# Softmax sums inverted on VectorE in the last blocks of a fused attention and feed-forward kernel, with the order of the last five blocks written anew

## The chip, the cores and the metric

The kernel runs on one core of a Trainium2 chip. The metric is device time in microseconds of one execution; of several runs the median is taken. Each core has TensorE (PE, matrix products into PSUM), ScalarE (ACT, functions such as the exponential), VectorE (DVE), GpSimd (POOL) and SyncE (SP, which here issues most DMAs). Each engine works through its own instructions strictly in the order in which the program lists them; semaphores make one wait for another.

## The reference

```python
x = A_x                                   # 1 x 2048 x 448, bf16
xn = _layernorm(x)                        # no scale, no shift
qkv = xn @ A_wqkv                         # 16 heads of 28
p = softmax(q @ k.T * 28 ** -0.5)         # per head, 2048 x 2048
s = (p @ v) @ A_wo
h = gelu(xn @ B_w1 + B_b1)                # 1792 wide
g = silu(h @ B_w2 + B_b2)
return x + s * g
```

There are 16 x 2048 x 2048 exponentials, and they are the bulk of the work.

## The kernel before

The sixteen heads form four groups `g` of four, and the 2048 queries four chunks `c` of 512. A pair (g, c) is a *block*; `ORD` lists the sixteen blocks in the order in which they run, numbered 0 to 15. A block has 64 *pieces*, one for each head of the group and each of the 16 key tiles of 128 keys: a score matmul (`t_score`, line 1430) makes a 128x512 piece in one PSUM bank, and ScalarE takes the exponential of two or three pieces in neighbouring banks at once (`p_exps`, line 1486). A second matmul (line 1866, from `t_pv`) multiplies each exponentiated piece by the values `vaug`, which carry an extra column that yields the softmax sums, and adds it up in the one PSUM bank `acc` that a block has. Block 15 is handled in three parts of 256, 128 and 128 queries by functions of its own (`p_epi4`, `p_norm4`, `p_last`).

ScalarE does not make all exponentials. Some key tiles of a block (only those listed in `VT`, eight at most for each block) are taken as *late quads*, four pieces at a time: VectorE makes an approximate exponential by integer arithmetic on the bits (`p_apass`, line 1715), then two shifted copies of the four pieces (`p_expq`, line 1774), and the three are weighted with `vaug` and with scaled values `vs` in the second matmul. If a setting allows it, GpSimd first adds the two shifted copies (line 1787, four additions); the quad is then *merged*, and needs fewer matmuls. `NQ` gives for each block how many tries are made to take a late quad; a try comes to nothing when the piece is already too near.

When a block is finished, `p_epi` copies `acc` to SBUF in `E_sb` (line 1929, VectorE). The 4x512 sums then travel through DRAM so that they lie as 128x16 in `rs` (lines 1941 and 1943; for block 14 four direct DMAs, line 1938). GpSimd inverts them into `rc` with the power -1 (line 1945). `rc` goes back through DRAM (line 1947) and is spread over the partitions by four DMAs (line 1950) into `rb`, and GpSimd multiplies `E_sb` by it (line 1954), giving the normalized block in `qT`. All those DMAs are issued by SP. The output projection of a chunk (line 1964) needs all four groups of it; its results are multiplied by the gate on VectorE (line 1981), and leave with an accumulating DMA from GpSimd (line 1990) or, for the last chunks, after an addition of x on VectorE (line 1985) by SP (line 1987). The feed-forward part runs between the blocks: first layer (line 1278), GELU in one stretch (line 1326), second layer (line 1347) with its bias added at line 1353, and SiLU as a tanh on ScalarE (line 1363) with products on GpSimd (lines 1368 and 1370) or VectorE (line 1374).

The order of all this is made by a planner in the file itself, while the program is being built. Each step is a `_Task` with an engine, a reckoned duration and latency, and a priority; `run` always takes the step that can begin first by this reckoning, with priorities among those that begin at nearly the same time. A DMA is reckoned to land a `lag` after its issue: 4.0 us each for the steps of an epilogue, and `LAG` for blocks 12 and later. Nothing of the reckoned times is in the program, only the order on each engine and the waits. `BP` holds seventeen rows of twenty settings, named in `BPN`; `tune` loads a row when the first scores of a block are listed. Among them are `MG` (1: late quads may be merged on GpSimd), `PV0` and `PVC` (how far the second matmul may fall behind), `ND4` and `LQ` (how many quads may be under way), `JMAX` (how many late pieces may join a score group), `QLEAD` and `QDIST` (how long before its use a quad may or must be taken), `UR` and `SLACK` (urgency on TensorE) and `R3` (whether groups of three scores are made; at 4 the banks 2 and 3 of the ring are kept for them).

Of the kernel before, what the change touches and what calls it, by code (L numbers as in the profile page):

```python
# [8 lines left out]
ALU = mybir.AluOpType  # L9
ET = mybir.EngineType  # L10

PE, ACT, DVE, POOL, SP = ET.PE, ET.Activation, ET.DVE, ET.Pool, ET.SP
# [38 lines left out]
)  # L51
NQ = (5, 11, 13, 13, 12, 7, 11, 10, 16, 3, 16, 15, 12, 13, 12, 14)
QLEAD, QDIST = 0, 12
JMAX, DQ, LQ, ND4, LU = 2, 3, 2, 3, 3
PV0, PVC, MP = 12, 4, 0.3
# [35 lines left out]
PVN = 2  # L91
OWN2 = 0
EA = 0
LAG, ONS = 3.0, 1.0
LNR = 1
G3P = 0
PATH = {(1, 2): 'D', (1, 3): 'D', (2, 0): 'D', (2, 1): 'D', (2, 2): 'D', (2, 3): 'D'}
# [30 lines left out]
class _Kernel:  # L128
# [1457 lines left out]
    def p_late(self):  # L1586
# [4 lines left out]
        for b in range(NBLK):  # L1591
            i = 0
            while True:
                if i:
                    K.nq_read = b
                at = 64 * b - QLEAD + (i * (64 - QDIST) // NQ[b] if i else 0)
                yield ("until", lambda: K.next_m >= at)
                K.nq_read = b
                if i >= NQ[b]:
                    break  # L1600
# [323 lines left out]
    def p_epi(self, b):  # L1924
        K = self
        g, c = ORD[b]
        E = K.E_sb[:, b % 2, :]
        tE = K.b_E[b % 2]
        yield _Task(DVE, lambda eng: eng.tensor_copy(E, K.acc[:, :]), [K.b_acc], [tE], 0.7, 0.0, 0)
        K.E_done = b  # L1930
        K.copying = False
        yield ("until", lambda: K.late_on)
        lag = LAG if b >= NBLK - 4 else 4.0
        src = bass.AP(tensor=K.E_sb, offset=DH * 1024 + 512 * (b % 2), ap=[[32 * 1024, 4], [1, 512]])
        if b == NBLK - 2:
            for j in range(4):
                one = bass.AP(tensor=K.E_sb, offset=(32 * j + DH) * 1024 + 512 * (b % 2), ap=[[1024, 1], [16, 32], [1, 16]])
                K.dma(SP, lambda eng, j=j, one=one: eng.dma_start(K.rs[32 * j:32 * j + 32, :], one), K.s_r[1],
                      reads=[tE], writes=[K.b_srs] if j == 3 else [], land=max(K.now, tE.tw) + lag)
        else:  # L1940
            K.dma(SP, lambda eng: eng.dma_start(K.sums.ap(), src), K.s_r[0], reads=[tE], writes=[K.b_sums],
                  land=max(K.now, tE.tw) + lag)
            K.dma(SP, lambda eng: eng.dma_start(K.rs[:, :], K.sums.ap().rearrange("j (i k) -> (j i) k", k=16)), K.s_r[1],
                  reads=[K.b_sums], writes=[K.b_srs], land=K.b_sums.tw + lag)
        yield _Task(POOL, lambda eng: eng.tensor_tensor(K.rc[:, :], K.rs[:, :], K.mone[:, 0:1].to_broadcast([128, 16]), ALU.pow),  # L1945
                    [K.b_srs, K.b_pads], [K.b_rc], 3.0, 0.05, 1)
        K.dma(SP, lambda eng: eng.dma_start(K.recs.ap().rearrange("j (i k) -> (j i) k", k=16), K.rc[:, :]), K.s_r[2],
              reads=[K.b_rc], writes=[K.b_recs], land=max(K.now, K.b_rc.tw) + lag)
        for j in range(4):
            h = K.dma(SP, lambda eng, j=j: eng.dma_start(K.rb[32 * j:32 * j + 32, :], K.recs.ap()[j].partition_broadcast(32)),  # L1950
                      K.s_r[3], reads=[] if j else [K.b_recs], writes=[] if j else [K.b_rb], land=0.0)
        K.mark(h, [K.b_recs], [K.b_rb], K.b_recs.tw + lag + 0.6)
        dst = K.qT[:, g, c * 512:(c + 1) * 512]
        yield _Task(POOL, lambda eng: eng.tensor_tensor(dst, K.rb, E, ALU.mult), [K.b_rb, tE], [K.b_onT[g][c]], 1.15, 0.05, 1,  # L1954
                    port=True)
        K.on_done[b] = True
# [111 lines left out]
```

## Time and profile before

| | |
|---|---|
| time, median of 3 runs | 420.60 us (420.59 to 420.64) |
| the profiled execution | 420.68 us |
| its span | 418.88 us |
| busy: PE, ACT, DVE, POOL | 396.6, 404.8, 345.0, 188.2 us |
| the power on GpSimd, line 1945 | 15 of 2.997 us in the mean, 45.0 us |
| merging additions on GpSimd, line 1787, in the last 165 us | 20, most of 1.15 us |
| copies of `acc`, line 1929, blocks 10 to 14 | end at 302.5, 322.5, 343.3, 370.1, 390.7 us |
| last exponential | ends at 411.5 us |

The span runs from the first to the last instruction of one profiled execution; its time includes what lies around the span. Lines such as `L1945 POOL TENSOR_TENSOR rc<-rs,mone 128x16` name the source line, the engine, the operation, what is written from what, and the tile. "Idle before" is time for which the engine stood still just before an instruction, with the instruction or DMA that released it. Consecutive instructions of one engine overlap in the records, so their pace is read from start to start. The busy time of a TensorE instruction is modelled.

### The profile page before, as it was taken

Reading aid. Unit: us, or ns where it says so; the run is one execution under the profiler, and the core shown is the slowest. Engines: PE = TensorE matmul, PEld = TensorE weight load, DVE = VectorE, ACT = ScalarE, POOL = GpSimd, SP = SyncE. Lnnn points to the kernel's source line nnn. Section 1 sums busy time; section 2 is a strip of 40 time slices with the busy share of each in tenths; the row PEclk is TensorE's granted clock in tenths of the full one; section 3 lists DMA queues with packets and bytes.
Section 4 is the critical chain, followed back from the end, with each engine's and each line's share of the span. In section 5 each row is a group of like instructions: output and inputs, shape, how many; then the busy total and the mean of one; then the engine's idle time right before and its main releaser. Section 6 shows DMA issues by size and latency. Waiting matters only on the chain.

```text
span 418.9 us, 9607 instructions
## 1 busy us (share of the span) xinstructions
PE 396.6 (95%) x3640; PEld 133.8 (32%) x3666; DVE 345.0 (82%) x594; ACT 404.8 (97%) x412; POOL 188.2 (45%) x193
## 2 busy tenths in 40 slices
PE   6899999999999999999999999999999999999996
PEld 4543223332222222222223443232222322323443
DVE  8968899997786899999894126799998899899387
ACT  5999999999999999999999999999999999999994
POOL 6571333237769271203331424408325618880660
PEclk9999999999999999999999999999999999999999
DMA  8701000000001000000230000000010001211052
GB/s 270 264 2 40 3 3 27 12 19 15 26 2 27 0 2 30 2 27 15 60 112 26 27 1 2 2 2 14 15 27 3 9 22 23 49 46 28 2 126 80
DMA packets 15952, 15.29 MB, mean 36 GB/s; under 512 B 7129, under 2 KB 12993, under 8 KB 15874
## 3 DMA queue, kind: packets, MB, share of 16 engines
q1 hardware_dynamic: 15042, 13.07, 10.8%
q0 software_dynamic: 576, 0.92, 1.5%
q8 instruction: 29, 0.48, 0.5%
q10 hardware_dynamic: 288, 0.69, 0.4%
q14 instruction: 17, 0.14, 0.1%
HBM read 12.59 MB, written 2.93 MB: 37 GB/s over the span
## 4 chain that ended last, share of the span: by engine, by line
PE 60%; ACT 23%; issue 8%; DVE 6%; POOL 2%; ACTq 0%; POOLq 0%; DVEq 0%
PE ring L1430 18%; PE acc L1866 13%; ACT P L1486 13%; PE ring L1278 8%; ACT h L1486 7%; PE ring L1347 7%; PE ring L923 2%; PE misc L923 2%; PE misc L1347 2%; ACT xnT L1486 2%; PE misc L1278 1%; PE ring L1217 1%; PE acc L1064 1%; PE misc L1217 1%; PE ring L1964 1%
## 5 line engine op out<-in xcount | busy, mean ns | idle before, releaser
L1486 ACT ACTIVATE P<-ring 128x1024 bf16<-128x1024 f32 (+1 forms) x238 | 252.1, 1161 | 1.8 <-PE ring L1430 0.7
L1430 PE MATMUL ring<-qT,kT 32*128 32x512 bf16 (+2 forms) x1045 | 140.9, 357 | 9.7 <-ACT P L1486 2.0
L1486 ACT ACTIVATE h<-ring 128x1024 bf16<-128x1024 f32 (+1 forms) x80 | 87.2, 1191 | 0.1
L1430 PEld LDWEIGHTS ring<-qT,kT 32*128 32x128 bf16 x1045 | 38.0, 91 | 144.0 <-ACT P L1486 81.0
L1945 POOL TENSOR_TENSOR rc<-rs,mone 128x16 f32<-128x16 bf16 x15 | 45.0, 2997 | 32.7 <-DMA rs<-sums 24.5
L1866 PE MATMUL acc<-P,vaug 128*32 128x512 bf16 (+2 forms) x618 | 54.3, 351 | 0.0
L1278 PE MATMUL ring<-xnT,w 128*128 128x512 bf16 x169 | 46.0, 381 | 1.4 <-issue 0.8
L1486 ACT ACTIVATE xnT<-ring 128x1024 bf16<-128x1024 f32 (+2 forms) x38 | 43.0, 1172 | 2.0 <-PE ring L1430 1.4
L1954 POOL TENSOR_TENSOR qT<-x_sb,E_sb 128x512 bf16<-128x512 f32 x15 | 19.6, 1304 | 51.9 <-PE acc L1866 21.2
L1347 PE MATMUL ring<-w,h 128*128 128x448 bf16 x168 | 40.5, 355 | 0.3 <-DVE vaug L1715 0.3
L1430 PE MATMUL misc<-qT,kT 32*128 32x512 bf16 (+1 forms) x107 | 40.7, 382 | 0.0
L1866 PE MATMUL acc<-h,vaug 128*32 128x512 bf16 x230 | 27.9, 384 | 0.0
L1172 POOL TENSOR_TENSOR qsq<-qT 128x512 bf16<-128x512 bf16 x12 | 12.5, 1040 | 33.2 <-DVE qT L1166 30.6
L1715 DVE TENSOR_SCALAR x_sb<-ring 128x512 uint16<-128x512 f32 x38 | 25.7, 685 | 1.7 <-PE ring L1430 1.3
L1715 DVE TENSOR_SCALAR x_sb<-misc 128x512 uint16<-128x512 f32 x30 | 20.6, 686 | 4.7 <-PE misc L1430 4.0
L1368 POOL TENSOR_TENSOR h<-w 128x448 bf16<-128x448 bf16 x12 | 12.7, 1058 | 23.8 <-DVE h L1774 14.5
L1715 DVE TENSOR_SCALAR h<-ring 128x512 uint16<-128x512 f32 x33 | 22.3, 685 | 0.0
L1278 PEld LDWEIGHTS ring<-xnT,w 128*128 128x128 bf16 x180 | 14.7, 97 | 23.8 <-issue 8.3
L1799 POOL TENSOR_SCALAR vs<-vaug 128x128 bf16<-128x128 bf16 x32 | 9.5, 297 | 21.2 <-DVE w L1774 18.6
L1866 PEld LDWEIGHTS acc<-P,vaug 128*32 128x32 bf16 x618 | 13.3, 95 | 15.1 <-issue 12.6
L1347 PEld LDWEIGHTS ring<-w,h 128*128 128x128 bf16 x168 | 12.3, 97 | 17.9 <-issue 10.6
L1262 DVE CAST h<-ring 128x512 bf16<-128x512 f32 x21 | 14.4, 685 | 4.4 <-PE ring L1278 4.3
(265 smaller groups left out, 700.4 us busy)
## 6 DMA issues: line engine op xcount, KB each, us to landing
x_sb<-recs SPq DMA_DIRECT2D x60, 64.0 KB, 2.0
w<-in_B_w_dram SPq DMA_DIRECT2D x1, 1568.0 KB, 7.2
w<-in_B_w_dram SPq DMA_DIRECT2D x1, 1344.0 KB, 8.4
x_sb<-in_A_x_dram SPq DMA_DIRECT2D x2, 448.0 KB, 4.6
out_dram<-in_A_x_dram SPq DMA_DIRECT2D x2, 448.0 KB, 9.8
out_dram<-h POOLq DMA_DIRECT2D x4, 224.0 KB, 4.4
out_dram<-h SPq DMA_DIRECT2D x8, 112.0 KB, 1.7
h<-in_A_wqkv_dram SPq DMA_DIRECT2D x3, 168.0 KB, 4.9
```

The source lines that it names most:

```text
L923: return eng.matmul(bank, w[:, k, g * 128:(g + 1) * 128], K.xnT[:, k, c * 512:(c + 1) * 512], start=(k == 0), stop=(k == KT - 1))
L1172: yield _Task(POOL, lambda eng: eng.tensor_tensor(qs, qb, qb, ALU.mult), [qr], [tq], 1.1, 0.05, 2, port=True)
L1262: yield _Task(DVE, lambda eng: eng.tensor_copy(dst, bank), [tok], wr, 0.69, 0.0, 2)
L1278: return eng.matmul(bank, K.w1[:, k, ft * 128:(ft + 1) * 128], K.xnT[:, k, c * 512:(c + 1) * 512], start=(k == 0), stop=(k == KT - 1))
L1347: ins = eng.matmul(ps, hv[:, ft, t * 128:(t + 1) * 128], K.w2[:, ft, :], start=(ft == 0), stop=(ft == FT - 1))
L1368: yield _Task(POOL, lambda eng, o=o, t=t: eng.tensor_tensor(o, sg[:, t, :], fb[:, t, :], ALU.mult), [K.b_sig[c % 2], K.b_fsb[c % 2]], [K.b ...
L1430: return eng.matmul(dst, K.kT[32 * j:32 * j + 32, g, t * 128:(t + 1) * 128], K.qT[32 * j:32 * j + 32, g, c * 512 + q0:c * 512 + q0 + nq], ...
L1486: return eng.activation(reg[:, i0:i0 + n, :], K.ring[:, b0:b0 + n, :], ACTF.Exp, scale=SM_SCALE)
L1715: yield _Task(DVE, lambda eng: eng.tensor_scalar(K.part(u, k).bitcast(dt.uint16), K.like(u, bank), SM_SCALE * LOG2E * 128.0, (127.0 - EXP_ ...
L1866: return eng.matmul(K.acc[32 * j:32 * j + 32, q0:q0 + nq], w, ap[:, col:col + nq] if len(ap.shape) == 2 else ap[:, col // 128:(col + nq) / ...
L1945: yield _Task(POOL, lambda eng: eng.tensor_tensor(K.rc[:, :], K.rs[:, :], K.mone[:, 0:1].to_broadcast([128, 16]), ALU.pow), [K.b_srs, K.b_ ...
L1954: yield _Task(POOL, lambda eng: eng.tensor_tensor(dst, K.rb, E, ALU.mult), [K.b_rb, tE], [K.b_onT[g][c]], 1.15, 0.05, 1, port=True)
```

## The change

From block 11 on (`RCB = 11`), the sums of a block are inverted by `reciprocal` on VectorE and not by the power on GpSimd; the planner reckons 0.25 us for it, with priority 2, where the power had 3.0 us and priority 1. Block 15 has an epilogue of its own and is not concerned, so four inversions move, those of blocks 11 to 14. `LAG` goes from 3.0 to 3.5, so that the planner reckons longer DMAs in the epilogues of blocks 12 to 14. The rows 11 to 15 of `BP` get other settings, and `NQ` for blocks 13 and 14 becomes 15 and 9. Since the planner's order follows from all these, the order on every engine can differ from the place on where row 11 is loaded. The computation is the same.

```diff
-    (0, 0.227, 10, 0.102, 12, 6, 0.124, 9, 17, 0.113, 1, 6, 4, 8, 1.0, 1.3, 75, 28, 0, 3.77),
-    (0, 5.612, 12, 0.137, 9, 10, 0.124, 4, 18, 0.4, 1, 4, 8, 2, 0.413, 1.275, 90, 16, 4, 5.0),
-    (1, 6.265, 18, 0.121, 15, 2, 3.663, 5, 6, 0.064, 1, 3, 8, 3, 0.519, 2.119, 60, 38, 0, 3.491),
-    (0, 2.077, 13, 0.119, 14, 3, 0.232, 9, 16, 0.334, 1, 1, 9, 12, 0.378, 1.28, 88, 16, 0, 6.0),
-    (1, 4.0, 5, 0.1, 6, 6, 0.298, 3, 18, 0.206, 1, 3, 8, 21, 0.202, 0.491, 48, 20, 2, 1.109),
+    (0, 0.186, 10, 0.156, 21, 9, 0.124, 9, 17, 0.251, 5, 6, 3, 8, 1.0, 4.428, 75, 28, 0, 3.77),
+    (1, 5.612, 31, 0.218, 9, 8, 0.059, 6, 18, 0.316, 1, 3, 8, 4, 0.682, 1.275, 98, 12, 1, 5.0),
+    (1, 6.265, 5, 0.121, 25, 10, 3.663, 5, 6, 0.064, 1, 1, 10, 3, 0.13, 2.119, 60, 38, 1, 3.491),
+    (0, 1.756, 13, 0.029, 14, 7, 0.232, 9, 16, 0.03, 1, 7, 9, 12, 0.211, 4.579, 52, 24, 0, 6.0),
+    (1, 4.0, 5, 0.1, 6, 7, 0.298, 3, 18, 0.206, 1, 3, 8, 21, 0.202, 0.491, 18, 20, 2, 1.109),
...
-NQ = (5, 11, 13, 13, 12, 7, 11, 10, 16, 3, 16, 15, 12, 13, 12, 14)
+NQ = (5, 11, 13, 13, 12, 7, 11, 10, 16, 3, 16, 15, 12, 15, 9, 14)
...
-LAG, ONS = 3.0, 1.0
+LAG, ONS = 3.5, 1.0
+RCB = 11
...
-        yield _Task(POOL, lambda eng: eng.tensor_tensor(K.rc[:, :], K.rs[:, :], K.mone[:, 0:1].to_broadcast([128, 16]), ALU.pow),
-                    [K.b_srs, K.b_pads], [K.b_rc], 3.0, 0.05, 1)
+        if b >= RCB:
+            yield _Task(DVE, lambda eng: eng.reciprocal(K.rc[:, :], K.rs[:, :]), [K.b_srs], [K.b_rc], 0.25, 0.0, 2)
+        else:
+            yield _Task(POOL, lambda eng: eng.tensor_tensor(K.rc[:, :], K.rs[:, :], K.mone[:, 0:1].to_broadcast([128, 16]), ALU.pow),
+                        [K.b_srs, K.b_pads], [K.b_rc], 3.0, 0.05, 1)
```

## The prediction

> **What bounds the kernel now.** I read the page's busy times first, then busy time by stretch, with the stretches cut where VectorE copies a finished block's sums out of PSUM (`E_sb<-acc`, line 1929).
>
> ```profile
> span 418.9 us, 9607 instructions
> PE 396.6 (95%) x3640; PEld 133.8 (32%) x3666; DVE 345.0 (82%) x594; ACT 404.8 (97%) x412; POOL 188.2 (45%) x193
> ```
> ```profile
> core 0: us, PE busy (x) PEld busy (x) DVE busy (x) ACT busy (x) POOL busy (x), PEclk, DMA share, GB/s
> 302.40:322.40 20.00, 19.98 (x181) 5.79 (x179) 19.82 (x32) 20.00 (x21) 6.96 (x5) 1.00 0.06 16
> 322.40:343.20 20.80, 19.82 (x203) 6.26 (x201) 17.54 (x27) 20.80 (x20) 10.03 (x8) 1.00 0.05 15
> 343.20:370.00 26.80, 25.89 (x207) 7.84 (x207) 24.49 (x40) 25.83 (x28) 21.13 (x18) 1.00 0.18 28
> 370.00:390.70 20.70, 20.42 (x239) 6.23 (x237) 19.20 (x33) 20.59 (x21) 8.75 (x5) 1.00 0.15 38
> 390.70:411.50 20.80, 19.70 (x347) 9.65 (x350) 12.92 (x23) 19.34 (x19) 11.16 (x8) 1.00 0.32 76
> ```
>
> ScalarE bounds it, TensorE close behind. From the place where the change begins to act (block 11, scored from about 300 us), ScalarE is idle 0.97 + 0.11 + 1.46 = 2.54 us. That is all that better ordering can win; more comes only if VectorE takes exponentials over. VectorE is idle 0.18 + 3.26 + 2.31 + 1.50 = 7.25 us in the first four stretches. POOL has room except in the third, and the granted clock is 1.00 throughout.
>
> Next the chain that ended last, at the end of block 14, and the waits in that place:
>
> ```profile
> 389.99 0.69 DVE E_sb L1929
> 390.68 0.61 DVE xnT L1774
> ...
> 392.54 1.15 POOL wk L1787
> 393.69 1.81 issue
> 395.53 2.91 POOL rc L1945
> 398.44 3.09 POOL wk L1787 x2
> 401.66 0.40 PE acc L1866 x8
> ```
> ```profile
> PE acc L1866 <- POOL wk L1787: 0.9, 1, 0.9
> ```
> ```profile
> 402.93 1.45 ACT L1486 ACTIVATE xnT<-ring 128x1536 bf16<-128x1536 f32 x1 [0.92 <-PE ring L1430]
> 409.99 1.02 ACT L1486 ACTIVATE P<-ring 128x1024 bf16<-128x1024 f32 x1 [0.38 <-PE ring L1430]
> ```
>
> The power (`rc`) stands in POOL's queue between the second and third of the four adds that merge block 15's late quad. POOL waits there 1.81 us for the DMA of the sums, works 2.91 us, then makes the other two adds. TensorE stands 0.91 us for them with the next scores queued behind, and ScalarE then idles 0.92 us. This is the one place where the power lies on the path. After 309, 329, 351 and 373 us the chain does not pass through it.
>
> How much VectorE already takes over comes from the matmuls that read the scaled values `vs`, which only late quads use: 8 for a plain quad, 4 for a merged one (columns: the stretch, busy PE with its count, weight loads, POOL).
>
> ```profile
> 302.40:321.70 19.30, 2.01 (x24) 0.54 (x24) 0.00 (x0) 1.00 0.06 17
> 322.40:342.60 20.20, 4.56 (x48) 1.16 (x48) 0.00 (x0) 1.00 0.05 16
> 343.20:369.40 26.20, 0.78 (x8) 0.21 (x8) 0.00 (x0) 1.00 0.19 29
> 370.00:390.70 20.70, 5.02 (x64) 1.70 (x64) 0.00 (x0) 1.00 0.15 38
> 390.70:411.50 20.80, 0.40 (x8) 0.15 (x8) 0.00 (x0) 1.00 0.32 76
> ```
>
> So 3, 6, 2 (merged), 8 and 1 (merged, half-width matmuls) quads in blocks 11 to 15: 20.
>
> **The change part by part.** Sums go against the profiled execution: span 418.88, time 420.68, so 1.80 around the span; that is 0.08 above the median, 420.60.
>
> *Power out of POOL.* Four of the fifteen powers go (blocks 11 to 14; block 15 has none): 4 x 3.0 = 12 us of POOL, of which 0.92 of ScalarE's idle time is on the path. Without it the four adds run from 391.43 to about 396.1 in place of 401.5, 4 us before TensorE reaches them; late next are ScalarE and TensorE themselves. **-0.92.** Between nothing and -0.92.
>
> *Earlier normalized block 14.* Its sums land at 395.5 either way. Then 0.26 in place of 2.91, the store (398.47 to 399.91 now), four broadcast loads from SP (1.71 plus some 2), and POOL's multiply, which now runs at 405.12 behind the adds and two output transfers of its queue. It can be done by about 402.5, not 406.4. The output matmuls (line 1964) that need it crowd 405.9 to 409.3, just ahead of the 0.38 idle at 409.99; spread out they let that go. **-0.38**, between -0.38 and 0.
>
> *Reciprocal on VectorE.* No 128x16 reciprocal is in the trace; 128x128 takes 948 ns, and the smallest operation near it, the 128x2 aggregate, 161. In proportion: 161 + 787 x 16/128 = 0.26 each, 1.05 for four, from 0.64 to 3.8 at the two rows. It waits in order for a DMA. For blocks 11 to 13 the sums are there 3.5 us after the copy (302.5 to 306.0 in block 10, where POOL waited only for them), and the order reckons 7 or 8, so nothing queued behind it waits. For block 14 it reckons 3.5 and the trace says 4.85, so up to 1.35 us in order. VectorE idles there 5.31 us before the line-1353 addition at 396.59. **0**; if the 7.25 us of cover are used up, +1.05.
>
> [...]
>
> *Longer reckoned transfers* (3.0 to 3.5) issue nothing new; they place the consumers later in the queues. SP's own order stays sums, reciprocals, broadcasts. **0**, by the slack above; bounds -0.4 to +0.4, the smaller of the two stalls.
>
> *Five rows anew.* Three things in them have a price. (a) Block 12 no longer keeps two banks for groups of three scores (R3 4 to 1). In 321.31 to 343.83 there are ten triples at 1.33 and ten pairs at (22.52 - 13.3)/10 = 0.92; ten triples as fifteen pairs cost +0.47, while block 13 (R3 0 to 1) may win that back. I take **+0.2**, bounds -0.47 and +0.47. The freed banks also let late scores come faster: from 330.8 to 336.0 they used one bank, 1.29 apart. (b) Block 12's quads may be merged on POOL (MG 0 to 1). A merge saves TensorE 4 matmuls, 0.22 us by the chain's step from 8 to 12 (0.55 to 0.76). For two quads -0.4 on TensorE, not on ScalarE: **0**. (c) Tries for late quads: block 13 gets 15 for 13, block 14 gets 9 for 12. One quad is 4 x 0.455 = 1.82 us of ScalarE and 6 x 0.6 = 3.6 of VectorE. The number follows from rules that the trace cannot replay: **0**, bounds -1.8 (one more fits the 7.25 idle) and +3.6 (two fewer).
>
> Sum: -0.92 - 0.38 + 0.2 = -1.10: 419.58 against the profiled time, **419.5** against the median.
>
> **The rivals.** *One quad more.* For it: VectorE's idle time, block 12's banks, and block 13 with 2 quads where blocks 12 and 14 have 6 and 8. Against: VectorE is 92 to 99% busy in the other stretches. 419.5 - 1.8 = **417.7**.
>
> *No gain.* New POOL merges in block 12 meet VectorE's shift passes (line 1774). The trace shows such meetings: 1.81 us beside an add at 354.15 where 0.68 is usual, and POOL's multiply taking 3.26 in place of 1.15 beside the shift passes that run to 388.9. Three shift passes lengthened by 1.1 eat 3.3 of the 3.26 idle in block 12's stretch, late scores come later and ScalarE loses the 1.1 again: **420.6**. [...]
>
> *Slower: quads go back to ScalarE.* Block 14 has 8 quads from 12 tries; at that rate 9 tries give 6, and block 13's 15 tries at 2 in 13 give none in return. One quad fewer is 421.3, two 423.1; the middle, **422.2**. It decides from one quad on, since 1.82 exceeds the 1.10 won. Against it: a block has at most 8 late quads, so the last four tries may have been empty.
>
> **How the numbers follow.** Changes under 0.2% (0.84 us) are about what a measurement of this kernel tells from none. Chances: forecast 0.31 (own range 418.9 to 420.1), one quad more 0.20, no gain 0.11, fewer quads 0.38. Most of the forecast's range lies under 419.76, so faster is 0.29 + 0.20 = 0.49. One quad fewer, at 421.3, is still just within the bound of 421.44, and I give it 0.05 of the 0.38: slower 0.33, same 0.02 + 0.11 + 0.05 = 0.18. The range runs from 417.3 to 422.6: it leaves out a second quad won, and two quads lost with nothing regained.
>
> **What would show it.** Right: no `rc` on POOL after 310 us, block 15's adds in one run ending by 397, no wait of TensorE on them, ScalarE's idle time after 302 down from 2.5 to about 1.2 us, 20 quads by the `vs` counts and 4 reciprocals of some 0.26 us. Wrong: another count of quads (1.8 us each), VectorE waiting for `rs`, shift passes over 1 us in block 12, or new ScalarE idle time behind scores.

## The result and the profile after

The changed kernel takes 419.35 us (median of 7 runs, 418.82 to 419.81), the kernel before beside it 420.62 us (7 runs): a ratio of 0.9964, 95% interval 0.9952 to 0.9976. It is faster by 1.27 us. The profiled execution is the lowest of the seven (418.82 us, span 417.0), while that of before was close to its median; so the two profiles stand 1.86 us apart, and 0.6 us of that belongs to the choice of the runs.

The span and the busy times on the page of the changed kernel:

```profile
span 417.0 us, 9616 instructions
PE 400.2 (96%) x3651; PEld 132.6 (32%) x3651; DVE 343.3 (82%) x592; ACT 405.9 (97%) x413; POOL 183.3 (44%) x197
```

TensorE's 400.2 us cannot be set beside the 396.6 of before, whose record lacks 26 matmuls: it has 3640 of them to 3666 weight loads, while pow_cheap and swap_late below, with the same program on TensorE, have 3666 of both.

Busy time by stretch in the changed kernel, cut at the copies of `acc` and, last, at the end of the last exponential (columns as in the same view of before):

```profile
302.09:320.60 18.51, 18.25 (x183) 5.30 (x181) 17.39 (x28) 18.32 (x19) 3.54 (x2) 1.00 0.07 17
320.60:345.71 25.11, 24.03 (x211) 7.09 (x207) 21.70 (x35) 25.11 (x25) 14.77 (x15) 1.00 0.06 13
345.71:371.49 25.78, 25.70 (x203) 7.74 (x202) 22.78 (x39) 25.72 (x27) 17.56 (x16) 1.00 0.19 30
371.49:389.68 18.19, 18.17 (x211) 5.71 (x210) 15.15 (x25) 17.96 (x18) 6.25 (x6) 1.00 0.17 43
389.68:410.13 20.45, 20.21 (x371) 10.28 (x369) 15.67 (x28) 20.45 (x19) 10.70 (x10) 1.00 0.35 84
```

ScalarE (fourth engine column) now stands still for 0.19 + 0.06 + 0.23 = 0.48 us in these stretches, where it was 2.54. Its busy time over the whole span rose from 404.8 to 405.9, since it makes four more pieces itself. That follows from the count of matmuls that read `vs` in the changed kernel (columns as in the same view of before):

```profile
302.10:320.40 18.30, 3.59 (x40) 0.96 (x40) 0.00 (x0) 1.00 0.07 17
320.60:345.50 24.90, 2.39 (x28) 0.74 (x28) 0.00 (x0) 1.00 0.06 13
345.70:371.30 25.60, 0.78 (x8) 0.21 (x8) 0.00 (x0) 1.00 0.19 30
371.50:389.50 18.00, 3.81 (x48) 1.27 (x48) 0.00 (x0) 1.00 0.17 43
389.70:410.10 20.40, 1.00 (x16) 0.43 (x16) 0.00 (x0) 1.00 0.35 84
```

They stand for 5, 4 (three plain, one merged), 2 merged, 6 and 2 merged half-width late quads: 19, one fewer than before (3, 6, 2, 8, 1). So the ledger from the copy of block 10 on, measured at the starts of the copies, reads: the five stretches last 109.65 us before and 108.72 after; 2.06 of idle time went, 1.13 of exponentials came; and what follows the last exponential is 6.9 us in place of 7.4. The remaining 0.44 us lie ahead of the first stretch (301.85 and 301.41), where the order is the same, and nearly all of it is there at the start already (the same small step of VectorE begins at 13.43 and 13.00 us); recip_only and recip_nowait below, whose orders are the same as each other, reached it at 301.38 and 302.04, so that is scatter.

GpSimd's work in the changed kernel at the place where the power stood:

```profile
386.53 2.26 POOL L1788 TENSOR_TENSOR xnT<-xnT,h 128x512 bf16<-128x512 bf16 x2 [11.73 <-DVE h L1775]
388.76 1.15 POOL L1958 TENSOR_TENSOR qT<-x_sb,E_sb 128x512 bf16<-128x512 f32 x1
389.87 2.25 POOL L1788 TENSOR_TENSOR xnT<-xnT,h 128x512 bf16<-128x512 bf16 x2
393.15 4.23 POOL L1788 TENSOR_TENSOR h<-h,x_sb 128x512 bf16<-128x512 bf16 x3 [1.02 <-DVE x_sb L1775]
397.32 0.87 POOL L1994 DMA_DIRECT2D out_dram<-h  x1
397.93 1.45 POOL L1788 TENSOR_TENSOR h<-h,x_sb 128x512 bf16<-128x512 bf16 x1
```

Block 15 now has eight adds for two quads (line 1788, 1787 before). They end at 399.4 and TensorE does not wait for them. VectorE's four reciprocals start at 329.97, 353.19, 380.23 and 393.37; only the last waits for its sums:

```profile
393.37 0.25 DVE L1947 RECIPROCAL rc<-rs 128x16 f32<-128x16 bf16 x1 [0.30 <-DMA rs<-E_sb]
```

### The profile page after: what moved, and what is told of

It reads as the page before. It is cut to its first block, busy times and chain, and to the rows that moved or that the text cites. A ratio compares the mean times of both kernels' runs of the same rounds, so it can differ in the third digit from the quotient of the medians.

```text
span 417.0 us, 9616 instructions
## 1 busy us (share of the span) xinstructions
PE 400.2 (96%) x3651; PEld 132.6 (32%) x3651; DVE 343.3 (82%) x592; ACT 405.9 (97%) x413; POOL 183.3 (44%) x197
## 4 chain that ended last, share of the span: by engine, by line
PE 72%; ACT 15%; DVE 7%; issue 5%; DMA 1%; ACTq 0%; DVEq 0%
PE ring L1431 23%; PE acc L1867 16%; PE ring L1279 9%; ACT P L1487 8%; PE ring L1348 7%; PE misc L1348 4%; PE ring L924 3%; ACT h L1487 3%; PE misc L924 3%; ACT xnT L1487 2%; PE misc L1279 2%; PE misc L1218 2%; PE ring L1218 1%; PE misc L1968 1%; ACT h L1327 1%
## 5 line engine op out<-in xcount | busy, mean ns | idle before, releaser
L1487 ACT ACTIVATE P<-ring 128x1024 bf16<-128x1024 f32 (+1 forms) x237 | 252.9, 1172 | 1.4 <-PE acc L1867 0.5
L1279 PE MATMUL ring<-xnT,w 128*128 128x512 bf16 x180 | 48.9, 382 | 0.0
L1949 POOL TENSOR_TENSOR rc<-rs,mone 128x16 f32<-128x16 bf16 x11 | 32.9, 2986 | 30.5 <-DMA rs<-sums 24.2
L1487 ACT ACTIVATE xnT<-ring 128x1024 bf16<-128x1024 f32 (+1 forms) x40 | 45.2, 1157 | 0.3 <-PE ring L1431 0.2
L1958 POOL TENSOR_TENSOR qT<-x_sb,E_sb 128x512 bf16<-128x512 f32 x15 | 17.3, 1156 | 42.9 <-PE acc L1867 22.8
L1348 PE MATMUL ring<-w,h 128*128 128x448 bf16 x140 | 33.6, 355 | 0.4 <-DVE vaug L1716 0.3
L1431 PE MATMUL misc<-qT,kT 32*128 32x512 bf16 (+1 forms) x88 | 32.6, 376 | 0.1
L1716 DVE TENSOR_SCALAR x_sb<-ring 128x512 uint16<-128x512 f32 x43 | 29.1, 686 | 2.6 <-PE ring L1431 2.1
L1348 PE MATMUL misc<-w,h 128*128 128x448 bf16 x84 | 21.8, 356 | 0.0
L1716 DVE TENSOR_SCALAR h<-ring 128x512 uint16<-128x512 f32 x31 | 20.9, 686 | 0.9 <-PE ring L1431 0.6
L1716 DVE TENSOR_SCALAR x_sb<-misc 128x512 uint16<-128x512 f32 x25 | 17.1, 685 | 4.7 <-PE misc L1431 4.0
```

The source lines that it names most:

```text
L1279: return eng.matmul(bank, K.w1[:, k, ft * 128:(ft + 1) * 128], K.xnT[:, k, c * 512:(c + 1) * 512], start=(k == 0), stop=(k == KT - 1))
L1348: ins = eng.matmul(ps, hv[:, ft, t * 128:(t + 1) * 128], K.w2[:, ft, :], start=(ft == 0), stop=(ft == FT - 1))
L1431: return eng.matmul(dst, K.kT[32 * j:32 * j + 32, g, t * 128:(t + 1) * 128], K.qT[32 * j:32 * j + 32, g, c * 512 + q0:c * 512 + q0 + nq], ...
L1487: return eng.activation(reg[:, i0:i0 + n, :], K.ring[:, b0:b0 + n, :], ACTF.Exp, scale=SM_SCALE)
L1716: yield _Task(DVE, lambda eng: eng.tensor_scalar(K.part(u, k).bitcast(dt.uint16), K.like(u, bank), SM_SCALE * LOG2E * 128.0, (127.0 - EXP_ ...
```

## The experiments

The expectations name theories. A: the power in GpSimd's queue makes adds late, which stops TensorE and then ScalarE. B: the gain comes from the new settings' order, not from the power. C: VectorE, which waits in order for the sums, is what costs. D: a re-planned order costs by itself, among other things by a quad more for block 15. E: `LAG` matters little, the additional quad does. F, formed after the first eight runs: the end follows from when GpSimd's adds for block 15 end, and with them its first part. G and H are stated where they appear.

All twelve runs in one table; each ratio is to runs of the kernel before on the same chip. "Zeros" counts the matmuls by a tile of zeros (line 1083 of the changed kernel): the planner inserts them where it reckons that TensorE has been idle lately.

| run | late quads 11 to 15 | zeros | last exponential ends | span | median us | ratio, 95% interval |
|---|---|---|---|---|---|---|
| before | 3 6 2 8 1 | 12 | 411.5 | 418.9 | 420.62 | |
| changed | 5 4 2 6 2 | 9 | 410.1 | 417.0 | 419.35 | 0.9964 (0.9952, 0.9976) |
| recip_only | 3 6 2 7 2 | 54 | 411.2 | 422.0 | 424.22 | 1.0069 (1.0053, 1.0086) |
| rows_only | 5 4 2 5 3 | 54 | 418.7 | 425.2 | 427.07 | 1.0137 (1.0111, 1.0163) |
| pow_cheap | as before | 12 | 409.2 | 416.5 | 418.54 | 0.9944 (0.9924, 0.9963) |
| swap_late | as before | 12 | 409.7 | 417.1 | 418.61 | 0.9960 (0.9947, 0.9974) |
| swap_all | as before | 12 | 409.9 | 417.3 | 418.86 | 0.9949 (0.9931, 0.9966) |
| pow_back | as changed | 9 | 411.2 | 418.1 | 420.30 | 0.9985 (0.9973, 0.9997) |
| recip_x4 | as changed | 9 | 410.6 | 417.5 | 419.44 | 0.9977 (0.9969, 0.9986) |
| recip_nowait | as recip_only | 54 | 411.9 | 422.6 | 424.45 | 1.0097 (1.0084, 1.0110) |
| lag30 | 5 4 2 6 3 | 51 | 418.4 | 426.4 | 427.93 | 1.0173 (1.0159, 1.0186) |
| lag30_q2 | 5 4 2 6 2 | 30 | 411.0 | 418.3 | 420.46 | 0.9985 (0.9972, 0.9999) |
| recip_nomerge | 3 6 2 7 2, last not merged | 36 | 409.9 | 420.7 | 422.74 | 1.0045 (1.0029, 1.0061) |
| after_nomerge | 5 4 2 6 2, last not merged | 9 | 412.6 | 419.1 | 421.48 | 1.0011 (0.9999, 1.0023) |

### One part of the change alone, order planned anew

recip_only: the kernel before with the reciprocal alone, settings and `LAG` as they were.

```diff
+RCB = 11
...
+        if b >= RCB:
+            yield _Task(DVE, lambda eng: eng.reciprocal(K.rc[:, :], K.rs[:, :]), [K.b_srs], [K.b_rc], 0.25, 0.0, 2)
```

> The kernel before with one part of the change: blocks 11 to 14 inverted on VectorE, the settings, NQ and LAG as before, the planner free to re-order. It keeps 20 late quads in the last five blocks. Theory A (the power in POOL's queue delayed the adds, and through them TensorE and ScalarE): 0.9 to 1.3 us faster than before, 419.3 to 419.7, ScalarE's idle time after 302 us down from 2.5 to about 1.2 us. Theory B (the gain is the new settings' order, the reciprocal does little by itself): within 0.4 us of before.

rows_only: the changed kernel with the power in all blocks.

```diff
-RCB = 11
+RCB = 16
```

> The changed kernel with the power back on POOL in all blocks, and the new settings, NQ and LAG 3.5 kept; the planner is free to re-order. 19 late quads in the last five blocks, as in the changed kernel. Theory A: no faster than before, 420.4 to 421.5, with a wait for POOL's adds or for the power near block 14's end. Theory B: 0.9 to 1.4 us faster than before, as the changed kernel is.

Both halves alone are slower than before, by 0.7% and 1.4%, though together they are faster. ScalarE's idle times over 0.15 us after 302 us in recip_only:

```profile
378.53 1.94 ACT L1487 ACTIVATE xnT<-ring 128x1024 bf16<-128x1024 f32 x2 [0.16 <-PE ring L1431]
393.69 5.48 ACT L1487 ACTIVATE P<-ring 128x1536 bf16<-128x1536 f32 x4 [1.32 <-PE acc L1867]
406.04 4.70 ACT L1487 ACTIVATE P<-ring 128x1536 bf16<-128x1536 f32 x4 [1.63 <-PE acc L1867]
```

Its last exponential ends no later than that of before (411.2 and 411.5), but 10.8 us follow it, not 7.4: 18 output matmuls (line 1968) are left at that time, in the kernel before 12. The matmuls of the stretch in recip_only, by group, from 380 us on:

```profile
L1348 PE MATMUL misc<-w,h 128*128 128x448 bf16 x25 | 6.3, 356 | 0.0
...
L1083 PE MATMUL acc<-ident,zero 128*128 128x128 bf16 x39 | 2.8, 219 | 0.0
```

In the kernel before there are 14 of the first (3.5 us) and none of the second there. The reciprocal of block 14 waits 4.59 us for its sums on VectorE. In rows_only ScalarE stands still 0.98 us before 385.66, 1.00 before 407.87 and 2.81 before 417.67. recip_only inverts as the changed kernel does, so what it loses against that kernel lies in the settings and `LAG` and in the order that follows from them. rows_only does not tell the power from the order: its last power (396.73 to 400.18) stands once more just ahead of four adds of block 15, which end at 405.53. TensorE's granted clock, 1.00 from 380 to 404 us in both, was 0.81 there from 404 to 427 us, a stretch that reaches past both spans, and 0.96 in the kernel before; in the mean of the span it was 0.992, in the kernel before 1.000. If all the time had followed the clock, that is (1 - 0.992) x 425.2 us, this would be an estimated 3.4 of the 6.3 us between the two spans.

### The order held, the power alone taken out

pow_cheap: the kernel before in its own order, and in blocks 11 to 14 GpSimd multiplies by a constant in place of the power (0.20 to 0.50 us).

```diff
+        if b >= 11:
+            fn = lambda eng: eng.tensor_scalar(K.rc[:, :], K.rs[:, :], 1e-17, 1e-17, op0=ALU.mult, op1=ALU.mult)
```

> The kernel before with its order on every engine kept as it is; in blocks 11 to 14 the power is replaced by a multiplication by a small constant on POOL, at the same place, so the inversion of the sums is left out there. Only the 2.9 us of each of these four powers go. Theory A: 0.9 to 1.3 us faster than before (0.92 from the adds, 0.38 from the earlier normalized block). Theory B: within 0.3 us of before, since another wait comes last.

swap_late: the kernel before in its own order, reckoned as if the power were still on GpSimd, but the instruction goes to VectorE's program as a reciprocal.

```diff
+        if b >= 11:
+            t.fn, t.at = lambda eng: eng.reciprocal(K.rc[:, :], K.rs[:, :]), DVE
```

> The kernel before with its order kept on every engine, except that in blocks 11 to 14 the power at its place in POOL's queue becomes a reciprocal on VectorE, put where VectorE's queue stands at that point of the order; settings, NQ and LAG as before, 20 late quads. Theory A (POOL's time was the cost, the reciprocal itself is covered): as with the cheap multiplication on POOL, 1.9 to 2.5 us faster than before, 418.2 to 418.9. Rival C (the reciprocal on VectorE costs by its time or by its wait for the sums): 1 us or more behind that, 419.5 to 421.

Both are faster than before, by 0.40% (swap_late) and 0.56% (pow_cheap), or 1.7 to 2.4 us. In swap_late the first copy starts as in before (301.81 and 301.85), so its stretches can be set side by side: that of block 13 is 0.81 us shorter, that of block 15 1.02, the others differ by at most 0.07. ScalarE's idle times over 0.15 us after 302 in the kernel before,

```profile
351.92 1.02 ACT L1486 ACTIVATE xnT<-ring 128x1024 bf16<-128x1024 f32 x1 [0.38 <-PE acc L1866]
357.14 1.02 ACT L1486 ACTIVATE xnT<-ring 128x1024 bf16<-128x1024 f32 x1 [0.53 <-PE ring L1430]
402.93 1.45 ACT L1486 ACTIVATE xnT<-ring 128x1536 bf16<-128x1536 f32 x1 [0.92 <-PE ring L1430]
409.99 1.02 ACT L1486 ACTIVATE P<-ring 128x1024 bf16<-128x1024 f32 x1 [0.38 <-PE ring L1430]
```

and in swap_late:

```profile
351.88 1.02 ACT L1487 ACTIVATE xnT<-ring 128x1024 bf16<-128x1024 f32 x1 [0.38 <-PE acc L1867]
408.19 1.02 ACT L1487 ACTIVATE P<-ring 128x1024 bf16<-128x1024 f32 x1 [0.38 <-PE ring L1431]
```

The 0.92 us of block 15 went, as theory A has it. So did the 0.53 of block 13, which the prediction had not put down to the power. What stood there in the kernel before, on GpSimd and on VectorE (start, length):

```profile
351.09 3.19 POOL L1945 TENSOR_TENSOR rc<-rs,mone 128x16 f32<-128x16 bf16 x1
353.99 1.40 POOL L1787 TENSOR_TENSOR vaug<-vaug 128x512 bf16<-128x512 bf16 x1
```
```profile
354.15 1.81 DVE L1774 TENSOR_SCALAR x_sb<-h 128x2048 uint16<-128x2048 uint16 x1
```

The power pushes the last add of a quad to 353.99, and a shift pass meets it. In swap_late the add runs at 351.05, and the same pass takes its usual time; the long pass, the idle time and the 0.81 us of block 13 went together (beside the idle time, the 26 pairs of this stretch follow each other 0.23 us sooner in sum):

```profile
354.11 0.68 DVE L1775 TENSOR_SCALAR x_sb<-h 128x2048 uint16<-128x2048 uint16 x1
```

The last 0.38 us of idle time stays in both experiments. The reciprocal of block 14 waits 4.06 us on VectorE in swap_late, and nothing comes later for it: in pow_cheap, where VectorE has no such wait, the same five stretches last as long to within 0.1 us.

### The order of the changed kernel, with its parts made dearer

pow_back: the changed kernel's order, and behind each reciprocal GpSimd gets a power again, whose result nobody reads.

```diff
+            K.emit(POOL, lambda eng: eng.tensor_tensor(K.junk[:, :], K.rc[:, :], K.mone[:, 0:1].to_broadcast([128, 16]), ALU.pow),
+                   [K.b_rc, K.b_pads], [K.b_junk], 0.0, 0.0)
```

> The changed kernel with its order kept, and one power more on POOL right behind each of the four reciprocals, into a scratch tile that nobody reads: it puts 12 us back on POOL and nothing else. Theory A: slower than the changed kernel by 0.5 to 1.3 us (419.9 to 420.7), block 15's merging adds again interrupted by 2.9 us. Theory B: within 0.3 us of the changed kernel's 419.35.

recip_x4: four reciprocals in place of each.

```diff
+                for i in range(3):
+                    eng.reciprocal(K.junk[:, i, :], K.rs[:, :])
```

> The changed kernel with its order kept and three more reciprocals of the same size, into a scratch tile, in front of each of the four: about 0.7 us more of VectorE at each of four places, 2.9 us in all. Theory A (VectorE's idle time covers the reciprocal): within 0.5 us of the changed kernel's 419.35. Rival C (VectorE is full): 1.5 to 2.9 us slower, 420.9 to 422.3.

With the power back, 0.95 us are lost by the medians (0.2% by the ratios, whose intervals overlap at the edge). The profiles put it where theory A has it: the stretch of block 15 lasts 22.16 us in place of 21.13, and the others differ by at most 0.13. TensorE waits for the adds again, and ScalarE for scores; the waits of TensorE and the idle time of ScalarE in pow_back:

```profile
PE acc L1869 <- POOL h L1790: 0.5, 1, 0.5
```
```profile
405.67 1.94 ACT L1489 ACTIVATE xnT<-ring 128x1024 bf16<-128x1024 f32 x2 [0.67 <-PE ring L1433]
```

That is mechanism A inside the changed kernel. Three reciprocals more each time delay the fourth by 0.39 us, not by the 0.7 expected, and the time stays: 419.44 against 419.35. So much more on VectorE at each place is covered.

### Is it VectorE's wait? recip_nowait

recip_only, but block 14's reciprocal reads a tile that is there already, so that VectorE doesn't wait for the sums; block 14 is then scaled by other numbers.

```diff
+            if b == NBLK - 2:
+                t.fn, t.free = lambda eng: eng.reciprocal(K.rc[:, :], K.b2b[:, 0:16]), True
```

> The kernel with the reciprocal alone (old settings, LAG 3.0; 424.2 us), its order kept; block 14's reciprocal reads a tile that has long been there instead of the sums, so VectorE does not wait 4.59 us for the DMA; block 14 is thus scaled by a wrong factor. Theory C (this in-order wait, which holds up the shift pass behind it, POOL's adds and ScalarE, is what made that kernel slower): 419.5 to 421.3. Rival D (its re-planned order costs the time by itself, among it one quad more that block 15 must merge in the last stretch): 423 to 424.5.

424.45 us, and ScalarE's 1.32 and 1.63 us are the same as in recip_only. Theory C falls for this kernel: a wait of 4.59 us in VectorE's queue cost nothing.

### The reckoned transfers: lag30 and lag30_q2

lag30: the changed kernel with the old `LAG`.

```diff
-LAG, ONS = 3.5, 1.0
+LAG, ONS = 3.0, 1.0
```

> The changed kernel with LAG back at 3.0, the planner free to re-order; 20 late quads, three of them in block 15. Theory C (a shorter reckoned transfer puts block 14's reciprocal into VectorE's queue too early): VectorE waits 1 to 4.6 us for the sums and the time is 420.5 to 423.5. Rival E (LAG matters little, the quad more counts): 417.5 to 419.5.

427.93 us, the slowest of all, against what theory E expected of `LAG`. Block 15 has three merged quads there. GpSimd's last adds and ScalarE in lag30:

```profile
403.07 2.50 POOL L1788 TENSOR_TENSOR kT<-kT,vaug 128x512 bf16<-128x512 bf16 x2
405.28 1.14 POOL L1994 DMA_DIRECT2D out_dram<-h  x1
405.89 2.81 POOL L1788 TENSOR_TENSOR kT<-kT,vaug 128x512 bf16<-128x512 bf16 x2
```
```profile
414.15 2.36 ACT L1487 ACTIVATE P<-ring 128x1536 bf16<-128x1536 f32 x2 [9.08 <-PE acc L1867]
```

lag30_q2 keeps that `LAG` and refuses block 15 a third quad.

```diff
+            if b == NBLK - 1 and K.late_left[b] + K.used15 >= 2:
+                return None
```

> The changed kernel with transfers reckoned at 3.0 us again (LAG 3.0), but block 15 limited to 2 late quads, so that its counts of late quads are those of the changed kernel (5, 4, 2, 6, 2) and only the order differs. In the run with LAG 3.0 alone block 15 had 3 merged quads, its last merging adds on POOL ended at 408.7 us, ScalarE stopped 9.08 us, 427.9 us. Theory F (what cost was the third quad of block 15, whose adds POOL made too late): block 15's adds end by 401 us again, ScalarE idle after 390 us under 1 us, total 418.8 to 421.0. Rival G (LAG 3.0 costs by itself, since VectorE's reciprocal then stands in its queue before block 14's sums have landed, 3.68 us in that run): that wait stays near 3 us and the total stays at 424 to 428.

420.46 us: 7.5 of the 8.6 us go with the third quad. Its adds end at 400.0, and ScalarE's idle time after 390 us is 0.18 + 0.46 until its exponentials are done. Rival G expected VectorE's wait for the sums to stay near 3 us and the time with it. The wait is 0.90 us here and was 3.68 in lag30, so it went together with the third quad, and this run does not separate the two; that a longer wait was free in swap_late and in recip_only speaks against G, in other orders. By the counts this kernel equals the changed one, and it is still 1.1 us slower by the medians (the intervals just overlap): so much is the order by `LAG` worth, with 21 zeros more.

### The adds taken away: recip_nomerge and after_nomerge

In both, block 15's two quads are not merged (first setting of row 15, `MG`), in recip_only and in the changed kernel.

```diff
-    (1, 4.0, 5, 0.1, 6, 6, 0.298, 3, 18, 0.206, 1, 3, 8, 21, 0.202, 0.491, 48, 20, 2, 1.109),
+    (0, 4.0, 5, 0.1, 6, 6, 0.298, 3, 18, 0.206, 1, 3, 8, 21, 0.202, 0.491, 48, 20, 2, 1.109),
```

> The reciprocal alone (settings and LAG of the kernel before, 424.2 us, adds of block 15 ending at 403.2, ScalarE idle 1.32 and 1.63 us behind scores), with the two late quads of block 15 not merged on POOL: POOL has no adds there, TensorE makes 8 more matmuls. Theory F (POOL's late adds hold block 15's first part and with it the end): the two idle times go, total 419.5 to 421.5. Rival H (the new order itself is worse, merged or not): ScalarE idle stays at 2.5 to 3 us, total 423.5 to 425.

> The changed kernel with the two late quads of block 15 not merged on POOL. Its adds now end at 399.4 us with no wait of TensorE on them, first part copied at 402.43. Theory F (the adds hold the first part): the copy comes up to 1 us earlier, 418.3 to 419.4 us. Rival (nothing waits for these adds any more, and eight half-width matmuls more, some 0.4 to 0.6 us, stand on TensorE while it is close to the bound): 419.6 to 421.5 us.

recip_nomerge comes between the two expectations: 422.74, 1.5 us better than recip_only. The idle time of 1.63 us at 406 is gone, that of 1.32 stays:

```profile
393.98 6.82 ACT L1487 ACTIVATE P<-ring 128x1536 bf16<-128x1536 f32 x5 [1.32 <-PE acc L1867]
```

The first part of block 15 is copied at 397.14 in place of 404.70, and the end is 1.3 us earlier in the span, no more. The exponentials end at 409.9, earlier than in the kernel before, and again 10.9 us follow, with 21 output matmuls. In after_nomerge the first part is copied at 397.15 in place of 402.43, and the kernel is 2.1 us slower than the changed one. ScalarE's idle times near its end:

```profile
405.17 1.02 ACT L1487 ACTIVATE xnT<-ring 128x1024 bf16<-128x1024 f32 x1 [0.30 <-PE ring L1431]
408.32 1.94 ACT L1487 ACTIVATE P<-ring 128x1024 bf16<-128x1024 f32 x2 [0.30 <-PE ring L1431]
411.59 1.02 ACT L1487 ACTIVATE P<-ring 128x1024 bf16<-128x1024 f32 x1 [1.33 <-PE ring L1431]
```

TensorE has no idle time over 0.15 us between 380 and 412 us there: it is full, as the rival said. So theory F falls as a rule. Late adds stand behind lag30, and taking them away gives back 1.5 of recip_only's 3.6 us. The rest of recip_only lies in the order of blocks 14 and 15 (block 14 ends at 391.49, in swap_late at 389.21, and one late quad fewer, 7 and not 8, is 1.82 us of that; feed-forward and zero matmuls stand where output matmuls stood). No run separates these.

### The swap for all blocks: swap_all

swap_late with all fifteen powers replaced (`if True:` in place of `if b >= 11:`).

> The kernel before in its own order, with all fifteen powers replaced in place by reciprocals on VectorE (the run with the last four replaced gave 418.6 us). Theory A (the power hurts where POOL's adds behind it are late, near the end, or where it pushes an add beside a shift pass): the eleven earlier powers lie in POOL's idle time, so within 0.3 us of the run with four, 418.3 to 418.9. Rival (earlier collisions of the same kind as in block 13, where a shift pass took 1.81 in place of 0.68 us, and 0.5 us each was to be had): one to three such places, 417.0 to 418.1. Against both: a VectorE that waits in order for sums that have not landed in the earlier blocks, 419.5 to 422.

418.86 us, the same as swap_late within its interval. The powers, 45.0 us of GpSimd's busy time in the kernel before, are gone and the time stays: the eleven earlier powers held up nothing that counts, as theory A expected. swap_late and swap_all have lower medians than the changed kernel, but their intervals overlap with that of the changed kernel, and that they beat it is not shown.

## Why the prediction came out right, step by step

The time was forecast at 419.5 and is 419.35, faster as forecast. The sum was -1.10; by the ledger above it is -2.06 of idle time, +1.13 of exponentials and -0.5 after them. So the total is right partly by luck: two errors of the working offset each other, an idle time that shrank by more than forecast and a quad that was lost.

- *Power out of POOL, -0.92.* Right, mechanism and size: -1.02 in block 15's stretch in swap_late, and about 0.9 lost again in pow_back. "This is the one place where the power lies on the path" is wrong: block 13 held another 0.81, through an add that the power pushed beside a shift pass. The chain of waits of before names only TensorE and ScalarE in that place, and the working stopped there. The prediction quoted that very pass, 1.81 us, as a sample of contention, without asking why the add ran so late.
- *Earlier normalized block 14, -0.38.* Failed: the idle time of 0.38 us is still there in pow_cheap and swap_late. In swap_late GpSimd's multiply of block 14 starts at 403.25 in place of 405.12, but the end of the exponentials came forward just as much, and in the kernel before no wait for this multiply is recorded at all. "Spread out they let that go" does not hold in that order; in the changed kernel the idle time is gone with the order itself.
- *Reciprocal on VectorE, 0.* Right: 0.24 to 0.25 us against 0.26, and covered even with four for each one. The wait for block 14's sums was put at up to 1.35 us and is 0.30; in other orders 4 us were free.
- *Longer reckoned transfers, 0, bounds ±0.4.* Mis-sized: 1.1 us with the counts held (lag30_q2), 8.6 us without (lag30). "Issue nothing new; they place the consumers later" overlooked that the next choices of the planner hang on it, the third quad of block 15 first.
- *Groups in block 12, +0.2.* By the listed groups, blocks 11 to 15 have 82 pairs, 25 triples and a single before, 83 pairs and 26 triples after: at 0.92 and 1.33 us a piece costs 0.455 us both times. Nothing, inside the bounds. (Ten triples as fifteen pairs would be 13.8 - 13.3 = +0.5 by the working's own figures, not +0.47.)
- *The number of quads, 0.* Failed by one, on the bad side: 19, not 20. The tries told half of it: block 14 with fewer went from 8 to 6 and block 13 with more stayed at 2, but blocks 11 and 12, whose tries stayed, went from 3 to 5 and from 6 to 4, and block 15 gained one. "92 to 99% busy in the other stretches" passed over block 15, where the working's own line has VectorE at 12.92 of 20.80 us. The quad was priced at 1.82 us, and ScalarE's work rose by 1.13. By the counts, a pair and a triple more and a single less are 1.77 us; but pairs and triples also follow each other sooner, every 0.927 and 1.332 us in the mean and not every 0.935 and 1.342, idle time left out, which takes back some 0.8. Why sooner, no run tells.
- *Rivals.* "Slower" was to decide "from one quad on, since 1.82 exceeds the 1.10 won". Its condition came true and it did not decide, since the new order won 2.06 us of the idle time, not 1.30. Of *no gain*, two shift passes in block 12 are longer (1.13 and 1.37 us), but they stand beside a product of the feed-forward part (line 1369) and the multiply of an epilogue (line 1958), not beside the new merging adds; VectorE still has 3.41 us free in that stretch, and ScalarE never stands still there.
- *What would show it.* No power on GpSimd after 310 and four reciprocals: seen. Adds in one run ending by 397: not in the changed kernel (two quads, 399.4), but in swap_late (390.65 to 395.1). ScalarE idle about 1.2 us: it is 0.48. Of the signs of being wrong, another count of quads was seen, and a wait of 0.30 us for `rs`. Shift passes over 1 us in block 12 were seen too, but say little, since the kernel before has two there as well (1.13 and 1.52 us).

What the prediction had no term for is the largest effect of all: with the planner free, the changed kernel loses 4.9 us without the settings and `LAG` (recip_only), 7.7 without the reciprocal (rows_only) and 8.6 without `LAG` (lag30). The new settings and `LAG` gain nothing over the bare swap in the old order (418.6); with the old settings planned anew the reciprocal costs 3.6 us. They belong together because they fit each other.

## What to carry to other kernels

When a file plans its own order, separate the edit from its re-planning: hold the order and swap the instruction alone, and then hold the new order and put the cost back. A slow instruction on an idle engine is worth a search for what stands behind it in its queue, and also for what that work then runs beside. Count what the planner hands out (late quads, filler matmuls) in every variant before blaming the operation that was edited.

## What the runs showed of the hardware

- An inversion of 128x16 took 2.89 to 3.37 us as a power on GpSimd in the kernel before (2.91 to 3.45 in pow_back and rows_only) and 0.24 or 0.25 us as a reciprocal on VectorE in the changed kernel; in a row, in recip_x4, each further reciprocal took 0.13 us (0.39 for three, start to start).
- In the kernel before ten shift passes that start beside a running addition or product of GpSimd (lines 1172, 1368, 1370 and 1787) take 0.89 to 1.81 us, where 0.68 is usual, and each ends 0.55 to 0.57 us after GpSimd's operation; the one of block 13 starts at 354.15 and ends at 355.96, the add runs from 353.99 to 355.39. Since 0.55 is close to the pass's own 0.68, the author reads this as waiting rather than sharing; no record shows the wait itself. Beside the multiply of an epilogue (line 1954, 386.67 to 389.93) it was the other way round: the three passes that start in its time take 0.68 or 0.69 us, and the multiply 3.26 in place of 1.15.
- A power is another matter: the 19 shift passes that run beside a power of GpSimd and nothing else of it, in the kernel before, take 0.68 or 0.69 us. In block 13 it is thus not the power itself that VectorE meets but the add that the power pushes back. One meeting of each kind, GpSimd's row first:

```profile
319.72 1.03 POOL L1368 TENSOR_TENSOR h<-w 128x448 bf16<-128x448 bf16 x1
319.79 1.51 DVE L1774 TENSOR_SCALAR kT<-h 128x2048 uint16<-128x2048 uint16 x1
329.13 3.00 POOL L1945 TENSOR_TENSOR rc<-rs,mone 128x16 f32<-128x16 bf16 x1
329.69 0.68 DVE L1774 TENSOR_SCALAR vaug<-vaug 128x2048 uint16<-128x2048 uint16 x1
```

- VectorE waited in order for 4.06 us (swap_late against pow_cheap) and 4.59 us (recip_only against recip_nowait) without any cost in time that these runs show: the five stretches last as long to within 0.1 us in the first two, and the medians of the other two are 424.22 and 424.45 us.
